# Dense head rows for the output projection and a second query block that ends in halves, in a fused pre-LN attention and gated feed-forward kernel

## The chip, the cores and the metric

The kernel runs on one NeuronCore of a Trainium2 chip, in one launch. The metric is the device time of that core in microseconds, as the median of several runs. The engines named below are TensorE (PE in the profile; its weight loads are PEld), VectorE (DVE), ScalarE (ACT), GpSimd (POOL) and SyncE (SP). SP issues nearly all DMAs of this kernel, one after the other, in the order in which the program was built.

## What is computed

One transformer block on x of 2048 rows and 640 columns (bf16), with 32 heads of 20 columns each, and a bilinear gated feed-forward layer of width 1728:

```python
def _A_ref(x, wqkv, wo):
    qkv = (x @ wqkv).reshape(B, S, 3, H, Dh).transpose(2, 0, 3, 1, 4)
    q, k, v = qkv[0], qkv[1], qkv[2]
    scores = jnp.einsum("bhqd,bhkd->bhqk", q, k) * (Dh ** -0.5)
    p = softmax(scores, axis=-1)
    o = jnp.einsum("bhqk,bhkd->bhqd", p, v)
    return o.transpose(0, 2, 1, 3).reshape(B, S, D) @ wo

def _B_ref(x, w_gate, w_up, w_down):
    return ((x @ w_gate) * (x @ w_up)) @ w_down

h  = x + _A_ref(layernorm(x), A_wqkv, A_wo)
h2 = h + _B_ref(layernorm(h), B_w_gate, B_w_up, B_w_down)
```

## The kernel before, in words

**Layout.** The heads are handled in eight groups of four (`NG = 8`, `HPG = 4`). Each head of 20 rows has a slot of 32 partitions, so a group fills the 128 partitions with 80 rows of use. The queries are cut into four blocks of 512 columns (`QB`), numbered 0 to 3.

**Attention.** A pass is one group against one query block or half of one. A list of passes, `segs`, is written out at the start: block 0 first (its first four groups in steps, while keys and values are still being made), then block 1 with all eight groups at 512 columns. Blocks 2 and 3 run their first two groups (`SPLIT_G = 2`) at 512 columns, and then the other six in two halves of 256: passes C and D for block 2, A and B for block 3. A half block's output can go on as soon as its own half is done.

The scores of a pass (keys on the partitions, queries on the columns) are cut into 683 tiles of 1536 columns in PSUM (`sc`, two buffers). For each tile, `emit_S` puts the score matmuls on TensorE and one exponential on ScalarE, into the SBUF tile `E`. Where `x_takes` says so, VectorE computes the exponential of the last 512 columns of a tile in four instructions (the tiles `xv`, `xt`, `xe`, called the x pieces here), and ScalarE's instruction is 1024 wide instead of 1536. In the last block `x_takes` asks `room()`: it adds up the TensorE work still to come by a table (`PE_NS`, `PART_NS`), compares it with the tiles that remain, and refuses a piece when less than `ROOM` is left over. `emit_AV` then multiplies `E` and `xe` with the values, into one PSUM tile `acc` per pass. The values carry a column of ones, so the sums of the exponentials come out as the 21st row of each slot.

**Normalising.** When a pass ends, VectorE copies `acc` to `asb`. `norm` sends the four rows of sums through DRAM (DMAs `sums`, `sums_all`), takes reciprocals four tiles later or more, sends these through DRAM again (`scr`, and four broadcasting DMAs `bc`), and seven tiles later VectorE multiplies (`times`) into `On[g]`, one tile for each group. The last groups of a half, named in `FAST`, do it on TensorE instead (`job_norm`).

**The rest of the block.** When all groups of a part (a block or half of one, list `due`) are normalised, `add_tail` queues three jobs: `job_out`, the output projection, which for each 128 rows and each half of the 640 columns (`out_mm`) sums over the eight group tiles, with `wo[g]` holding zeros between the slots; `job_glu`, the gate and up products over seven pairs of weight tiles (`glu_sum` at 512 columns, `glu_two` at 256); and `job_y`, the down projection and the store. A part of 512 columns loads each pair of weights once, a half block loads or holds them for its own 256 columns. `load_w` loads a pair while the one before is used, into two buffers. From the third block on, four of the seven pairs stay resident in the space of the old queries (`load_res`).

**Order.** The program is scheduled by the kernel itself while it is built: a loop over the tiles keeps estimates of each engine's time (`at`), and between score tiles `run_job` fills TensorE with chunks of the queued jobs as long as they fit before the next score tile is due. `later(n, fn)` does something n tiles later. `do(("spill", g), ...)` queues the copies of the queries to DRAM, which only a fallback at the end reads (`general`, entered when a check of the sums fails; it does not run on these inputs). When the tiles are done, `last_tail` finishes the last 256 rows on TensorE alone: `out_most` sums residual and groups 0 to 6, the last pass is normalised, `out_last` adds group 7, and then layer norm and feed-forward follow. The four halves of the down projection of the half block before (`held`) stand between them and hide the layer norm.

Of the kernel before, what the change touches and what calls it, by code (L numbers as in the profile page):

```python
# [29 lines left out]
NG = H // HPG  # L30
VS = DH + 1
# [11 lines left out]
SPLIT_G = 2  # L43
# [17 lines left out]
RES_STEPS = 3  # L61
WO_NS, SUMS_NS, ROOT_NS, ROWS_NS = 1500, 6000, 5000, 5000
# [6 lines left out]
PE_NS = {"out": 6000, "glu": 19500, "y": 3000}  # L69
PART_NS, TILE_NS, ROOM = 31500, 700, 5000  # L70
# [15 lines left out]
def kernel(  # L86
# [43 lines left out]
    wo = [const.tile([P, D], BF16, name=f"wo{g}") for g in range(NG)]  # L130
# [8 lines left out]
    On = [onp.tile([P, QB], BF16, name=f"on{g}") for g in range(NG)]  # L139
# [174 lines left out]
    def job_V(t, half):  # L314
        ps = bank()
        for c in range(KT):
# [12 lines left out]
            "C": (2, 0, HW), "D": (2, HW, HW), "A": (3, 0, HW), "B": (3, HW, HW)}  # L329
# [11 lines left out]
    TAILS = {0: [0], 1: [0], 2: [0, 2]}  # L341
    FAST = {("C", NG - 1), ("D", NG - 1), ("A", NG - 1), ("B", NG - 2)}
# [158 lines left out]
    def run_job(until):  # L501
# [9 lines left out]
        while cur["fresh"] or pe_free("F") + chunk() + SWITCH <= until:  # L511
            c = step()
            if c == FREE and cur["key"][0] not in ("spill", "load"):
                return run_job(until)
            if c in (None, NEXT, END, FREE):
                break
# [111 lines left out]

    def norm(s, asb):
# [11 lines left out]
        def back():  # L641
# [12 lines left out]
            def times(asb, bc, p, g, c0, w):  # L654
                nc.vector.tensor_tensor(On[g][:, c0:c0 + w], asb[:, 0:w], bc[:, 0:w], ALU.mult)
                done.add(("n", p, g))
# [32 lines left out]
    def job_norm(s, asb):  # L689
# [11 lines left out]
        nc.vector.tensor_tensor(On[g][:, c0:c0 + w], asb[:, 0:w], ps[:, 0:w], ALU.mult)  # L701
# [5 lines left out]
    def emit_AV(upto):  # L707
# [206 lines left out]
    def load_wo():  # L914
        for g in range(NG):
            nc.vector.memset(wo[g][:], 0.0)
            yield 230
            for j in range(HPG):
                h = HPG * g + j
                nc.sync.dma_start(wo[g][SLOT * j:SLOT * j + DH, :], A_wo[DH * h:DH * h + DH, :])  # L920
# [13 lines left out]
    def spill(g):  # L934
# [509 lines left out]
```

## Time and profile before

| What | Value |
|---|---|
| Median of 3 runs | 916.27 us (916.19 to 916.81) |
| The profiled execution | 916.05 us, span of its instructions 914.0 us |
| Granted TensorE clock, mean | 0.997 |
| Busy: PE, DVE, ACT, POOL | 817.5, 702.1, 866.2, 57.4 us |
| First and last exponential | from 15.6 to 869.9 us |
| DMA | 46.54 MB, mean 51 GB/s |

The span runs from the first to the last instruction; the time of a run has some 2 us more around it. Busy time of an engine counts its instructions and not its waits; a busy PE is not a PE at its peak. The chain that ended last is followed back from the last instruction, at each step to what released it. A line such as `L547 ACT ACTIVATE E<-sc` names the source line, the engine, the operation, and the tile written and read.

### The profile page before, as it was taken

How to read it: one execution, taken by the hardware profiler on the slowest of the kernel's cores; microseconds unless marked ns; L12 is line 12 of the kernel's file. 1: busy time of each engine (PE TensorE's matmuls, PEld its weight loads, DVE VectorE, ACT ScalarE, POOL GpSimd, SP SyncE). 2: the span in 40 equal slices, each digit the busy share in tenths (PEclk: the TensorE clock that was granted, in tenths of full speed). 3: DMA queues.
4: the chain of work that ended last, by engine and by line, in shares of the span. 5: the costliest groups of instructions: out<-in, count | busy, mean ns of one | idle time of the engine just before them, and what ended most of it. 6: DMA issues, size and time to landing. Idle time of an engine off the chain costs nothing.

```text
span 914.0 us, 20094 instructions
## 1 busy us (share of the span) xinstructions
PE 817.5 (89%) x8035; PEld 346.8 (38%) x8115; DVE 702.1 (77%) x1310; ACT 866.2 (95%) x719; POOL 57.4 (6%) x255
## 2 busy tenths in 40 slices
PE   8788999889989899899897888999998999998897
PEld 5233333222223222233232333434434445444575
DVE  8664349899999899899998999798998784542243
ACT  6999999999999999999999999999999999999931
POOL 4210000000001200000003000020001000010000
PEclk9999999999999999999999999999999999999999
DMA  6000011011025022212410022021411211201310
GB/s 195 17 14 1 1 27 27 14 24 37 4 61 149 13 71 72 64 49 90 160 28 14 20 70 68 19 54 49 117 51 42 73 28 51 57 15 50 80 44 18
DMA packets 74203, 46.54 MB, mean 51 GB/s; under 512 B 20380, under 2 KB 70440, under 8 KB 74104
## 3 DMA queue, kind: packets, MB, share of 16 engines
q1 hardware_dynamic: 74104, 45.20, 18.0%
q8 instruction: 65, 1.06, 0.5%
q14 instruction: 34, 0.28, 0.1%
HBM read 37.88 MB, written 7.30 MB: 49 GB/s over the span
## 4 chain that ended last, share of the span: by engine, by line
ACT 67%; issue 17%; PE 10%; DVE 4%; DMA 1%; POOL 1%; SPq 0%; ACTq 0%
ACT E L547 67%; PE sc L533 2%; PE f L1065 2%; PE f L1129 2%; PE acc L740 1%; DVE st L201 1%; PE mi L303 1%; PE mi L978 0%; PE f L1230 0%; PE mi L496 0%; DMA wu<-in_B_w_up_dram 0%; PE mi L317 0%; PE mi L1083 0%; DVE kT L310 0%; DVE vx L270 0%
## 5 line engine op out<-in xcount | busy, mean ns | idle before, releaser
L547 ACT ACTIVATE E<-sc 128x1536 bf16<-128x1536 f32 (+1 forms) x683 | 848.7, 1417 | 6.2 <-PE sc L533 5.9
L533 PE MATMUL sc<-qa,kT 32*128 32x512 bf16 (+1 forms) x1920 | 203.2, 340 | 28.6 <-ACT E L547 16.9
L533 PEld LDWEIGHTS <-kT 32*128 32x128 bf16 x2816 | 84.1, 91 | 244.6 <-issue 206.1
L740 PE MATMUL acc<-E,vx 128*32 128x256 bf16 (+1 forms) x2592 | 170.3, 326 | 1.7 <-DVE vx L270 1.2
L580 DVE TENSOR_SCALAR xv<-sc 128x512 f32<-128x512 f32 x167 | 115.0, 689 | 30.2 <-PE sc L533 26.5
L585 DVE SCALAR_TENSOR_TENSOR xe<-xt,xv 128x512 int16<-128x512 f32 x167 | 113.3, 682 | 1.0
L591 DVE SCALAR_TENSOR_TENSOR xt<-xt,xv 128x512 f32<-128x512 f32 x167 | 112.3, 681 | 0.5
L590 DVE SCALAR_TENSOR_TENSOR xt<-xv 128x512 f32<-128x512 uint16 x167 | 112.0, 683 | 0.3
L303 PE MATMUL mi<-lnT,wp 128*128 128x512 bf16 x279 | 83.3, 381 | 11.7 <-DVE qa L310 5.5
L740 PEld LDWEIGHTS <-vx 128*32 128x32 bf16 x2816 | 55.8, 95 | 66.4 <-issue 63.8
L533 PE MATMUL sc<-qb,kT 32*128 32x256 bf16 (+1 forms) x896 | 68.2, 288 | 8.1 <-ACT E L547 5.3
L1129 PE MATMUL mi<-wd,hh 128*128 128x320 bf16 x336 | 58.2, 301 | 1.6 <-DVE xr L1133 1.6
L740 PE MATMUL acc<-xe,vx 128*32 128x512 bf16 (+1 forms) x224 | 50.6, 332 | 0.0
L1129 PEld LDWEIGHTS <-hh 128*128 128x128 bf16 x448 | 38.7, 97 | 30.6 <-issue 18.7
L303 PEld LDWEIGHTS <-wp 128*128 128x128 bf16 x310 | 25.0, 97 | 55.9 <-issue 44.3
L310 DVE TENSOR_SCALAR kT<-mi,one_row 128x512 bf16<-128x512 f32 x30 | 22.5, 750 | 28.1 <-PE mi L303 24.7
L1065 PE MATMUL mi<-ln2T,wg 128*128 128x512 bf16 x128 | 38.0, 382 | 5.8 <-DVE u L270 5.2
L496 PE MATMUL mi<-kT,ident 128*128 128x512 bf16 x116 | 37.8, 386 | 5.5 <-DVE ln2T L270 1.0
L978 PE MATMUL mi<-wo,on 128*128 128x320 bf16 x224 | 40.5, 301 | 2.2 <-DVE xr L982 2.0
L1065 PE MATMUL mi<-ln2T,wu 128*128 128x512 bf16 x128 | 37.3, 382 | 4.3 <-DVE hh L1073 3.5
L1083 PE MATMUL mi<-ln2T,qa 128*128 128x256 bf16 x240 | 34.6, 274 | 4.1 <-DVE hh L1091 3.0
L207 POOL CAST mb<-mv 128x2 bf16<-128x2 f32 (+1 forms) x10 | 2.3, 231 | 528.6 <-DVE mv L202 410.9
(143 smaller groups left out, 645.0 us busy)
## 6 DMA issues: line engine op xcount, KB each, us to landing
wu<-in_B_w_up_dram SPq DMA_DIRECT2D x23, 320.0 KB
wg<-in_B_w_gate_dram SPq DMA_DIRECT2D x23, 320.0 KB
bc<-scr SPq DMA_DIRECT2D x80, 64.0 KB
qsp<-qa SPq DMA_DIRECT2D x8, 384.0 KB
xr<-in_A_x_dram SPq DMA_DIRECT2D x16, 160.0 KB
bc<-scr SPq DMA_DIRECT2D x76, 32.0 KB
out_dram<-xr SPq DMA_DIRECT2D x14, 160.0 KB
wd<-in_B_w_down_dram SPq DMA_DIRECT2D x13, 160.0 KB
```

The source lines that it names most:

```text
L303: nc.tensor.matmul(ps[:], lhsT=wslice(m, g, c), rhs=lnT[:, c, ch * QB:(ch + 1) * QB], start=(c == 0), stop=(c == KT - 1))
L496: nc.tensor.matmul(ps[:], lhsT=ident[:], rhs=kT[0][:, 0:BANK], start=True, stop=True)
L533: nc.tensor.matmul(sc[:, o:o + w], lhsT=kT[g][SLOT * j:SLOT * (j + 1), kt * P:(kt + 1) * P], rhs=q_of(g, b, c0, w)[SLOT * j:SLOT * (j + 1) ...
L547: exps = nc.scalar.activation(e[:, 0:n_act], sc[:, 0:n_act], ACT.Exp, bias=EXP_BIAS, scale=SM_SCALE)
L580: took = nc.vector.tensor_scalar(v[:], ps, X_SCALE, X_BASE, ALU.mult, ALU.max)
L585: nc.vector.scalar_tensor_tensor(e[:], t[:], X_R, v[:], ALU.mult, ALU.add)
L590: lambda: nc.vector.scalar_tensor_tensor(t[:], u, X_P, u, ALU.add, ALU.mult),
L591: lambda: nc.vector.scalar_tensor_tensor(t[:], t[:], X_Q, u, ALU.add, ALU.mult),
L740: nc.tensor.matmul(acc["t"][SLOT * j:SLOT * (j + 1), 0:w], lhsT=vx[kt][:, VS * h:VS * h + SLOT], rhs=e, start=(acc["n"][j] == 0), stop=(ac ...
L978: nc.tensor.matmul(ps[:, 0:HALF], lhsT=on[g][:, t * P:(t + 1) * P], rhs=wo[g][:, cs], start=(g == 0), stop=(g == NG - 1))
L1065: nc.tensor.matmul(ps[:, 0:n], lhsT=st["w", fp][k][:, c, f_cols(fp, f2)], rhs=st["ln2T"][:, c, c0:c0 + n], start=(c == 0), stop=(c == KT - 1))
L1129: nc.tensor.matmul(ps[:, 0:HALF], lhsT=st["hh"][f // 2][:, f % 2, t * P:(t + 1) * P], rhs=late["Wd"][f][:, cs], start=(f == 0), stop=(f == ...
```

## The change

It has two parts, and some constants that go with them.

**Dense rows.** The attention outputs of groups 0 to 6 (`OWN = 7`), 560 rows, are put one behind the other into five tiles of 128 rows (`NC = 5`) without the gaps of the slots. Group 7 keeps a slotted tile of its own (index 5), so the projection sums over six tiles instead of eight. VectorE multiplies a group below 7 into a staging tile `on` (two buffers), and SP moves each of its heads to the rows where they belong, in one DMA, or two where a head crosses from one tile to the next (`heads_of`). `times` marks such a group as done `ROWS_STEPS = 2` tiles later. `wo` is loaded in the same row order: five DMAs and four instead of 32, and two tiles zeroed instead of eight.

**Halves.** Block 1 runs its first four groups at 512 columns and then the other four in two halves (passes E and F), and its output, gate, up and down jobs come in two parts of 256 columns. Block 3 splits from its second group on instead of its third; block 2 stays as it was.

**Constants and order.** `room()` counts 4900 instead of 6000 for an output projection, and `ROOM` is 1000 instead of 5000. The spills of the queries come at fixed tiles (60 and four more for each group after block 0's part is queued) instead of in the queue of jobs. `asb` has three buffers instead of two. `rows_early`, the early load of the residual rows, waits for the second phase of memory to be open, and also covers the halves of block 1.

```diff
+OWN = NG - 1
+NC = -(-OWN * HPG * DH // P)
...
-SPLIT_G = 2
+SPLIT_G = {"1": 4, "2": 2, "3": 1}
...
+ROWS_STEPS, SPILL_AT = 2, 60
...
-PE_NS = {"out": 6000, "glu": 19500, "y": 3000}
-PART_NS, TILE_NS, ROOM = 31500, 700, 5000
+PE_NS = {"out": 4900, "glu": 19500, "y": 3000}
+PART_NS, TILE_NS, ROOM = 31500, 700, 1000
...
-    On = [onp.tile([P, QB], BF16, name=f"on{g}") for g in range(NG)]
+    On = [onp.tile([P, QB], BF16, name=f"on{c}") for c in range(NC + 1)]
...
+    nc.gpsimd.memset(On[NC - 1][:], 0.0)
...
+            "E": (1, 0, HW), "F": (1, HW, HW), "C": (2, 0, HW), "D": (2, HW, HW), "A": (3, 0, HW), "B": (3, HW, HW)}
...
-    segs += [("1", g, 0, NT, "only") for g in range(NG)]
-    for full, halves in ("2", "CD"), ("3", "AB"):
-        segs += [(full, g, 0, NT, "only") for g in range(SPLIT_G)]
-        segs += [(p, g, 0, NT, "only") for p in halves for g in range(SPLIT_G, NG)]
+    for full, halves in ("1", "EF"), ("2", "CD"), ("3", "AB"):
+        segs += [(full, g, 0, NT, "only") for g in range(SPLIT_G[full])]
+        segs += [(p, g, 0, NT, "only") for p in halves for g in range(SPLIT_G[full], NG)]
...
-    FAST = {("C", NG - 1), ("D", NG - 1), ("A", NG - 1), ("B", NG - 2)}
+    FAST = {("E", NG - 1), ("F", NG - 1), ("C", NG - 1), ("D", NG - 1), ("A", NG - 1), ("B", NG - 2)}
...
+    @contextmanager
+    def heads_of(g, c0, w):
+        if g == OWN:
+            yield On[NC][:, c0:c0 + w]
+            return
+        on = onp.tile([P, QB], BF16, name="on", tag="on", bufs=2)
+        yield on[:, 0:w]
+        for j in range(HPG):
+            a, end_ = DH * (HPG * g + j), DH * (HPG * g + j + 1)
+            while a < end_:
+                n = min(end_, (a // P + 1) * P) - a
+                r = SLOT * j + DH - (end_ - a)
+                nc.sync.dma_start(On[a // P][a % P:a % P + n, c0:c0 + w], on[r:r + n, 0:w])
+                a += n
...
             def times(asb, bc, p, g, c0, w):
-                nc.vector.tensor_tensor(On[g][:, c0:c0 + w], asb[:, 0:w], bc[:, 0:w], ALU.mult)
-                done.add(("n", p, g))
+                with heads_of(g, c0, w) as on:
+                    nc.vector.tensor_tensor(on, asb[:, 0:w], bc[:, 0:w], ALU.mult)
+                if g < OWN and now["i"] < n_tiles:
+                    later(ROWS_STEPS, lambda: done.add(("n", p, g)))
+                else:
+                    done.add(("n", p, g))
...
-                asb = parts[g] if kind == "copy" else nrm.tile([P, QB], F32, name="asb")
+                asb = parts[g] if kind == "copy" else nrm.tile([P, QB], F32, name="asb", bufs=3)
...
-            for g in range(NG):
-                nc.tensor.matmul(ps[:, 0:HALF], lhsT=on[g][:, t * P:(t + 1) * P], rhs=wo[g][:, cs],
-                                 start=(g == 0), stop=(g == NG - 1))
+            for c in range(NC + 1):
+                nc.tensor.matmul(ps[:, 0:HALF], lhsT=on[c][:, t * P:(t + 1) * P], rhs=wo[c][:, cs],
+                                 start=(c == 0), stop=(c == NC))
...
             for g in range(NG):
-                do(("spill", g), lambda g=g: spill(g))
+                later(SPILL_AT + 4 * g, lambda g=g: spill(g))
...
-            for g in range(NG - 1):
-                nc.tensor.matmul(ps[:, 0:HALF], lhsT=on[g][:, t * P:(t + 1) * P], rhs=wo[g][:, cs], start=False, stop=False)
+            for c in range(NC):
+                nc.tensor.matmul(ps[:, 0:HALF], lhsT=on[c][:, t * P:(t + 1) * P], rhs=wo[c][:, cs], start=False, stop=False)
...
-    due = [("0", range(NG), 0, [0, 1, 2, 3]), ("1", range(NG), 1, [0, 1, 2, 3]), ("C", range(SPLIT_G, NG), 2, [0, 1]),
-           ("D", range(SPLIT_G, NG), 2, [2, 3]), ("A", range(SPLIT_G, NG), 3, [0, 1])]
+    due = [("0", range(NG), 0, [0, 1, 2, 3]), ("E", range(SPLIT_G["1"], NG), 1, [0, 1]), ("F", range(SPLIT_G["1"], NG), 1, [2, 3]), ("C", range(SPLIT_G["2"], NG), 2, [0, 1]),
+           ("D", range(SPLIT_G["2"], NG), 2, [2, 3]), ("A", range(SPLIT_G["3"], NG), 3, [0, 1])]
```

More of the change, by code (lines that the diff above doesn't have):

```diff
@@ L2 @@
 from collections import deque
[L3 removed]
+from contextlib import ExitStack, contextmanager
 import concourse.bass as bass
@@ L129 @@
     huge = const.tile([P, 1], F32, name="huge")
-    wo = [const.tile([P, D], BF16, name=f"wo{g}") for g in range(NG)]
+    wo = [const.tile([P, D], BF16, name=f"wo{c}") for c in range(NC + 1)]
     N_SUMS = 16 * (NB * NG)
@@ L512, in run_job @@
             c = step()
-            if c == FREE and cur["key"][0] not in ("spill", "load"):
+            if c == FREE and cur["key"][0] != "load":
                 return run_job(until)
@@ L914, in load_wo @@
     def load_wo():
-        for g in range(NG):
[L916 to L920, printed above, removed]
+        for c in range(NC + 1):
+            rows = DH * HPG * OWN - c * P
+            if rows < P:
+                nc.vector.memset(wo[c][:], 0.0)
+                yield 330
+            if c < NC:
+                nc.sync.dma_start(wo[c][0:min(P, rows), :], A_wo[c * P:c * P + min(P, rows), :])
+            else:
+                for j in range(HPG):
+                    h = HPG * OWN + j
+                    nc.sync.dma_start(wo[c][SLOT * j:SLOT * j + DH, :], A_wo[DH * h:DH * h + DH, :])
             due = at["pe"] + WO_NS
@@ L1161, in rows_early @@
         key = b, ts[0]
-        if key in HELD_BY and key not in rows_in and all(("y",) + k in done for k in HELD_BY[key]):
+        if key in HELD_BY and key not in rows_in and ("open",) in done and all(("y",) + k in done for k in HELD_BY[key]):
             rows(b, ts)
```

33 lines of the change are left out of this document (18 added, 15 removed).

## The prediction

> **What bounds the kernel now.** I read the page first: busy shares, then the chain that ended last.
>
> ```profile
> span 914.0 us, 20094 instructions
> ...
> PE 817.5 (89%) x8035; PEld 346.8 (38%) x8115; DVE 702.1 (77%) x1310; ACT 866.2 (95%) x719; POOL 57.4 (6%) x255
> ...
> ACT 67%; issue 17%; PE 10%; DVE 4%; DMA 1%; POOL 1%; SPq 0%; ACTq 0%
> ```
>
> ScalarE is busy 95% of the span and carries 67% of the chain. The shares are an average, so the busy time by stretch comes next.
>
> ```profile
> core 0: us, PE busy (x) PEld busy (x) DVE busy (x) ACT busy (x) POOL busy (x), PEclk, DMA share, GB/s
> 200.00:250.00 50.00, 44.75 (x330) 13.39 (x335) 47.75 (x81) 50.00 (x43) 0.00 (x0) 1.00 0.12 27
> 500.00:510.00 10.00, 7.90 (x117) 3.11 (x117) 8.30 (x15) 9.51 (x9) 3.71 (x12) 0.83 0.09 25
> 550.00:600.00 50.00, 44.80 (x579) 19.34 (x584) 42.81 (x82) 50.00 (x42) 0.15 (x1) 1.00 0.17 44
> 650.00:700.00 50.00, 45.67 (x423) 20.08 (x423) 45.55 (x86) 50.00 (x42) 5.82 (x19) 1.00 0.33 85
> 750.00:800.00 50.00, 45.51 (x620) 25.24 (x615) 27.73 (x51) 49.16 (x39) 0.00 (x0) 1.00 0.19 50
> 800.00:850.00 50.00, 45.47 (x630) 24.61 (x635) 17.03 (x39) 50.00 (x38) 3.60 (x19) 1.00 0.12 30
> ```
>
> ACT is full in every stage, whether the passes are 512 columns wide (200 to 250) or 256 (550 to 600). So the length of the long middle is the ACT time of the exponentials plus the little that ACT waits:
>
> ```profile
> ACT E L547 <- PE sc L533: 5.9, 9, 1.1
> ```
>
> That is 5.9 us in nine waits. DVE takes a third of some exponential tiles away from ACT (the pieces x). In the last stage it is busy only 27.73 and 17.03 of 50 us: there the planner stops handing it pieces, because TensorE, at 45.5 of 50, would not finish the feed-forward work before the exponentials end. Freed TensorE time in the last block is worth something only through more such pieces. After the last exponential TensorE alone sets the end:
>
> ```profile
> 868.83 1.08 ACT E L547
> 869.91 0.04 issue
> 869.95 0.40 PE acc L740 x6
> ...
> 870.59 0.95 PE f L1230 x7
> ...
> 876.15 7.67 PE f L1129 x56
> ```
>
> **The change part by part.**
>
> *More pieces for DVE.* The order in which the built programs stand shows 683 exponential tiles in both, of which 168 are 1024 wide before and 179 after; the x pieces go from 167 to 178. By query block they go from 26, 55, 55, 31 to 27, 52, 55, 44. So 11 tiles more lose a third, 13 more of them in the last block, where DVE had room.
>
> ```profile
> L547 ACT ACTIVATE E<-sc 128x1536 bf16<-128x1536 f32 x515 | 717.2, 1520 | 5.7 <-PE sc L533 5.5
> L547 ACT ACTIVATE E<-sc 128x1024 bf16<-128x1024 f32 x168 | 178.2, 1100 | 0.5 <-PE sc L533 0.5
> ```
>
> 1520 - 1100 = 420 ns each, so 11 x 0.42 = **-4.6 us** on the path. Each piece costs DVE four instructions:
>
> ```profile
> L580 DVE TENSOR_SCALAR xv<-sc 128x512 f32<-128x512 f32 x167 | 115.0, 689 | 30.2 <-PE sc L533 26.5
> ```
>
> 13 x 4 x 0.69 = 36 us over the last 210 us or so. DVE had 22 and 33 us free in the two stretches above, so this is hidden; without that room the pieces would hold score banks and the gain would go.
>
> *Six products for eight in the output projection.* 28 halves in the middle and 4 at the end lose two matmuls each. One costs 0.95/7 = 0.136 us by the chain row of L1230. The 56 in the middle free 7.6 us of TensorE beside a full ACT: worth nothing themselves, they pay for the pieces. The 8 at the end lie on the path. The order also shows that 14 matmuls of the third down projection (L1129) leave the tail: 7 now stand before the last products with E, where TensorE waited for the last exponential
>
> ```profile
> 869.95 0.40 PE L740 MATMUL acc<-E,vx 128*32 128x256 bf16 x6 [0.52 <-ACT E L547]
> ```
>
> and 7 right behind them, still on the path. At 7.67/56 = 0.137 us each the tail loses 8 + 7 = 15 matmuls: **-2.0 us**. Bounds: the 7 moved ahead have only 0.52 us of wait to fill, so the rest may push the last products: -1.1 - 0.5 = -1.6 at the small end, -2.1 at the large one.
>
> *Halving.* Groups 4 to 7 of block 1 and group 1 of block 3 go through in halves. Scores and products with E of one tile, in 512 and in 256 columns:
>
> ```profile
> 424.65 0.39 PE L533 MATMUL sc<-qa,kT 32*128 32x512 bf16 x3
> ...
> 424.98 0.62 PE L740 MATMUL acc<-E,vx 128*32 128x512 bf16 x8
> ```
>
> ```profile
> 748.74 0.40 PE L533 MATMUL sc<-qb,kT 32*128 32x256 bf16 x6
> ...
> 761.26 0.62 PE L740 MATMUL acc<-E,vx 128*32 128x256 bf16 x16
> ```
>
> 0.39 against 0.40 and 0.62 against 0.62: over some 107 tiles 1 us of TensorE, beside ACT. Nothing.
>
> *Rows by DMA.* Each normalised group below 7 now goes to a staging tile, and four or five DMAs on SP put its heads into the dense rows: 193 issues. SP executes in order, and one place in this trace shows what a busy SP does:
>
> ```profile
> 752.18 0.32 SPq L649 DMA_DIRECT2D scr<-ri  x1
> ...
> 753.59 2.60 SPq L652 DMA_DIRECT2D bc<-scr  x4
> ...
> 756.23 0.42 SPq L1036 DMA_DIRECT2D wu<-in_B_w_up_dram  x1
> ...
> 759.21 0.50 SPq L636 DMA_DIRECT2D sums<-asb  x1
> 759.73 0.99 PEld L1083 LDWEIGHTS <-wu 128*128 128x128 bf16 x10 [1.31 <-DMA wu<-in_B_w_up_dram]
> 759.73 1.27 PE L1083 MATMUL mi<-ln2T,wu 128*128 128x256 bf16 x10 [1.03 <-DMA wu<-in_B_w_up_dram]
> 760.82 0.35 SPq L637 DMA_DIRECT2D sums_all<-sums  x1
> ...
> 761.44 1.45 ACT L547 ACTIVATE E<-sc 128x1536 bf16<-128x1536 f32 x1 [0.84 <-PE sc L533]
> 761.64 0.42 DVE L655 TENSOR_TENSOR on<-asb,bc 128x256 bf16<-128x256 f32 x1
> ```
>
> A weight load issued 4.05 us after the reciprocal's DMA landed late; TensorE stood 1.03 us and ACT lost 0.84 of it. Two new chances for the same:
>
> First, the output projection reads rows that may not be there. The loop counts a group as done ROWS_STEPS = 2 tiles after its multiply. A tile takes 50/42 = 1.19 us, so that is 2.4 us. What is needed: multiply 0.42, four issues ahead of the last, and 760.82 - 759.21 = 1.61 from the last issue to its landing. Issues cost 0.65 (2.60/4 above) or less:
>
> ```profile
> 429.42 1.71 SPq L652 DMA_DIRECT2D bc<-scr  x4
> ```
>
> 1.71/4 = 0.43. So 0.42 + 4 x 0.43 + 1.61 = 3.75 us, or 4.6 with the slow issue. Group 6 fills chunks 3 and 4, so three matmuls (0.4 us) run first: a wait of 3.75 - 2.4 - 0.4 = 0.95 to 1.8 us, of which ACT loses 0.2 less. By the build's order the gap between group 6's rows and the projection is the bare two tiles in two half blocks (block 2's second, block 3's first), three and four tiles in block 1's, ten or more elsewhere. Two full waits, and at three tiles 0 to 0.6: **+1.8 us**, between 0 (if DVE runs ahead of TensorE) and 3.8.
>
> [...]
>
> Second, block 1's two halves each load all their feed-forward weights, five pairs a half (block 2 holds four of seven resident), and use them about 4 to 7 tiles later instead of 9 to 12. The load above needed 759.73 - 756.23 = 3.5 us, or three tiles, so most are in time; I take one wait of 0.84 less a bit, **+0.5 us**, between 0 and 4 x 0.84 = 3.4, for those that stand right behind five row DMAs.
>
> *The rest costs nothing.* The zeroing on POOL stands before a wait that hides it:
>
> ```profile
> 3.75 0.30 POOL L190 MEMSET vx<- 128x12 bf16 x1
> 7.49 0.88 POOL L195 COPY wp<-E 128x640 bf16<-128x640 bf16 x1 [3.44 <-DMA E<-in_A_wqkv_dram]
> ```
>
> Fewer wo loads and memsets fall in a stretch where ACT is full (200 to 250), as do the q spills, moved ahead by some 40 tiles: only the fallback reads them, and SP then has 9 tiles between weight loads.
>
> **Sum.** -4.6 - 2.0 + 1.8 + 0.5 = -4.3 us. The profiled execution took 916.05 us (span 914.0 and 2.05 around it), 0.22 under the median 916.27 of the three runs, so 911.75 on its basis and 912.0 on the median's; I say **911.8 us**. The likeliest case's own range is 909.5 to 914.
>
> **Rivals.**
>
> *Clean.* DVE finishes its multiplies early, the rows are always there: 916.05 - 6.6 = 909.4 us. For it: DVE often stands idle in the last block. Against: the bare two tiles twice.
>
> *SP becomes the bound of the second block (slower).* Place: the halves of block 1, where ten pairs of weight loads, some 100 row and sum DMAs and the output stores queue in order. Every missed load costs 0.84 us of ACT as at 759.73, more if a store or a multiply ahead is late too. It decides from 6.6/0.84 = 8 such misses on; with all ten plus 3.8 us of row waits it is 916.05 - 6.6 + 8.4 + 3.8 = 921.7 us. Against: SP had room, and the one miss before stood behind a 2.60 us run of issues.
>
> *The pieces are not worth their ACT time.* The last block is then held by TensorE (45.5 of 50 us) and not by ACT: only the tail's 2.0 us remain, less 1.8 for rows: 915.9 us, no change. Against: ACT is at 50.00 there.
>
> *The array's clock falls more often.* Between 500 and 510 us the granted clock was 0.83 and ACT was busy 9.51 of 10: 0.49 us lost. The change takes away TensorE work (56 matmuls, and filler matmuls besides), so such dips could multiply; 13 of them would eat 6.4 us: about 916 us. The planner still places fillers, so I think this unlikely. [...]
>
> **How the numbers follow.** Forecast 0.55, clean 0.20, pieces worth nothing 0.08, SP as the bound 0.10 (a third of it still at no change, between 8 misses and fewer), clock 0.03, something else slower 0.04. A measurement here tells 0.2% (1.8 us) from no change: faster is below 914.4, slower above 918.1. Faster: 0.55 + 0.20 and a part of the SP case, 0.79; same: 0.12; slower: 0.09. Range 908.6 to 915.8: below, the clean case with the tail's and the pieces' own uncertainty; above, the forecast with its row waits at their upper end and three late loads (-6.6 + 3.8 + 3 x 0.84 = -0.3).
>
> **What would show it.** Right: 179 tiles of 1024 columns and ACT at 50 of 50 us with fewer us between the first and last exponential, by about 4.6 less new waits; the piece from the last exponential to the end shorter by 2.0; TensorE waits of about 1 us at the first output projection of block 2's second half and block 3's first, released by a DMA of the row tile. Wrong: ACT idle growing by over 4 us in total, PE waits for wu or wg in block 1's halves in more than two places, DVE waiting for DMAs of the staging tile, or a granted clock under 0.97 in more than one stretch of 50 us.

## The result, and the profile after

The changed kernel takes 923.78 us (median of 6 runs, 921.33 to 927.14) against 916.23 us (915.72 to 916.81) for the kernel before in the same comparison: a ratio of 1.0087 [1.0063, 1.0111]. It is 7.6 us slower, and 12 us above the forecast. The profiled execution took 922.27 us with a span of 920.0.

The page of the changed kernel, its busy shares and its chain, and the waits of ScalarE:

```profile
span 920.0 us, 21921 instructions
...
PE 816.3 (89%) x8743; PEld 366.3 (40%) x8810; DVE 728.0 (79%) x1367; ACT 864.2 (94%) x719; POOL 63.2 (7%) x256
...
ACT 47%; PE 23%; issue 13%; DVE 12%; DMA 2%; POOL 1%; SPq 1%; DVEq 0%; ACTq 0%
```

```profile
ACT E L550 <- PE sc L536: 11.2, 14, 1.8
...
ACT E L550 <- PE acc L763: 3.9, 7, 1.3
```

ScalarE is busy for 2.0 us less than before: the shorter tiles are there. But its share of the chain has dropped from 67% to 47%. It waits 11.2 us for scores where it waited 5.9, and there is a second row that the kernel before does not have: seven waits, 3.9 us, for products with E that still hold an E buffer. The same stretches as before (PE, PEld, DVE, ACT, POOL busy, granted clock):

```profile
core 0: us, PE busy (x) PEld busy (x) DVE busy (x) ACT busy (x) POOL busy (x), PEclk, DMA share, GB/s
200.00:250.00 50.00, 42.62 (x306) 12.76 (x308) 46.35 (x75) 47.84 (x41) 0.00 (x0) 0.98 0.10 29
550.00:600.00 50.00, 44.07 (x626) 23.89 (x626) 44.16 (x81) 49.23 (x42) 0.00 (x0) 1.00 0.39 98
750.00:800.00 50.00, 44.03 (x603) 22.40 (x605) 43.43 (x79) 48.28 (x40) 0.00 (x0) 1.00 0.16 42
800.00:850.00 50.00, 44.34 (x589) 21.29 (x594) 31.83 (x63) 47.63 (x38) 6.29 (x19) 0.97 0.13 31
```

ACT was at 50.00 in three of these four and now loses 0.8 to 2.4 us in each. VectorE has taken on its pieces in the last block (43.43 and 31.83 for 27.73 and 17.03). After the last exponential the chain reads:

```profile
876.45 1.08 ACT E L550
...
877.96 1.06 PE mi L1160 x7
...
879.16 0.68 PE f L1261 x5
...
883.81 5.77 PE f L1160 x42
```

Five products for seven in each half, 42 down matmuls for 56 with seven ahead of the projection. From the last exponential to the end of the span it is 42.5 us, 44.1 before.

The whole difference, between two profiled executions: the exponentials end at 877.5 us instead of 869.9, 7.6 later; the tail is 1.6 shorter; that is the 6.0 us of span. Eleven shorter tiles save 4.6 us of the first. ScalarE's idle time in front of exponentials, summed from the 61st tile on, rose from 1.7 to 11.5 us; 10.7 of these are waits of over 0.15 us, which the lines below show in brackets.

The rest, 2.4 us, lies in ScalarE's busy time, which fell by 2.0 us and not by 4.6. Without a gap, a whole exponential ends 1.34 us after the one before it in both kernels, and the two overlap by some 0.1 us. Behind a gap nothing overlaps, and it takes 1.45 us beside the gap. The changed kernel has 28 exponentials behind a gap where the kernel before has 8, so about 20 x 0.11 = 2.2 us. The exponentials themselves did not become slower.

**Where the 11.5 us lie.** The first wait of over 1 us:

```profile
243.71 0.69 DVE L674 TENSOR_TENSOR on<-asb,bc 128x512 bf16<-128x512 f32 x1
...
244.46 0.69 DVE L583 TENSOR_SCALAR xv<-sc 128x512 f32<-128x512 f32 x1
...
245.06 0.68 DVE L594 SCALAR_TENSOR_TENSOR xt<-xt,xv 128x512 f32<-128x512 f32 x1
...
245.71 0.69 DVE L775 COPY asb<-acc 128x512 f32<-128x512 f32 x1
246.46 0.61 PE L763 MATMUL acc<-E,vx 128*32 128x512 bf16 x8 [0.78 <-DVE asb L775]
246.93 4.17 ACT L550 ACTIVATE E<-sc 128x1536 bf16<-128x1536 f32 x3 [1.26 <-PE acc L763]
...
252.34 1.02 ACT L550 ACTIVATE E<-sc 128x1024 bf16<-128x1024 f32 x1 [1.24 <-PE sc L536]
```

A pass has ended, and its accumulator must be copied out before the next pass may use the bank. The copy stands in VectorE's order behind a normalising multiply and two steps of pieces. TensorE stands 0.78 us for it, and ScalarE, out of E buffers, 1.26. Seven waits for products with E at pass ends make the 3.9 us. At five of them (3.3 us) the products start within 0.1 us of the end of the copy, as here; at 613 and 814 us (0.6 us) the copy had ended 0.6 and 0.7 us before. The second wait of 1.24 comes 5 us later and has another cause, shown below. One of the two places where I had forecast a wait for rows:

```profile
794.45 0.41 DVE L674 TENSOR_TENSOR on<-asb,bc 128x256 bf16<-128x256 f32 x1
...
794.90 3.75 SPq L644 DMA_DIRECT2D on<-on  x5
...
799.93 0.43 PE L1009 MATMUL mi<-wo,on 128*128 128x320 bf16 x2 [1.12 <-DMA on<-on]
...
800.81 2.41 ACT L550 ACTIVATE E<-sc 128x1536 bf16<-128x1536 f32 x2 [1.78 <-PE sc L536]
...
803.72 1.02 ACT L550 ACTIVATE E<-sc 128x1024 bf16<-128x1024 f32 x1 [0.50 <-PE sc L536]
...
805.47 1.45 ACT L550 ACTIVATE E<-sc 128x1536 bf16<-128x1536 f32 x1 [0.72 <-PE sc L536]
```

Five issues take 3.75 us, 0.75 each. ScalarE loses 1.78 here and 1.21 at the other place (674 us, where TensorE waited 0.71 for the rows): 3.0. And again two more waits follow, 0.50 and 0.72. What they and the 1.24 have in common is the clock. Windows of 3.41 us before and after each fall of the granted clock, of the changed kernel:

```profile
245.07:248.48 3.41, 1.91 (x17) 1.00 0.07 18
248.48:251.89 3.41, 3.19 (x16) 0.50 0.06 11
...
661.50:664.91 3.41, 2.50 (x23) 1.00 0.05 9
664.91:671.74 6.83, 6.47 (x34) 0.50 0.60 165
798.03:801.44 3.41, 1.81 (x12) 1.00 0.04 8
801.44:804.85 3.41, 3.38 (x33) 0.50 0.03 5
```

(PE busy in us, its matmuls, granted clock, DMA.) TensorE was not idle ahead of these falls; it was busy 1.91, 2.50 and 1.81 of 3.41 us. One window at half clock follows, or two, in which the same work takes longer (the products of E over 512 columns take 619 ns on average from 248.48 to 251.89 us, 384 from 240 to 248.48) and the scores come late: 3.5 us of ScalarE behind the three. So 11.5 = 3.9 (pass ends) + 3.0 (rows) + 3.5 (behind clock falls) + 1.1 (small waits). This goes by the place of each wait; what a fall costs by itself is tested behind the third set.

The expectation of rows6, below, puts the middle fall down to the rows. But it came at 664.91 us, 9 us ahead of the row wait at 673.6. The window ahead of it holds two waits of TensorE, 0.46 us for VectorE (hh) and 0.70 us for ScalarE. That the change brought these is not shown.

### The profile page after: what moved, and what is told of

Its sections match the earlier page's. It is cut to its first block, busy times and chain, and to the rows that moved or that the text cites. A ratio compares the mean times of both kernels' runs of the same rounds, so it can differ in the third digit from the quotient of the medians.

```text
span 920.0 us, 21921 instructions
## 1 busy us (share of the span) xinstructions
PE 816.3 (89%) x8743; PEld 366.3 (40%) x8810; DVE 728.0 (79%) x1367; ACT 864.2 (94%) x719; POOL 63.2 (7%) x256
## 4 chain that ended last, share of the span: by engine, by line
ACT 47%; PE 23%; issue 13%; DVE 12%; DMA 2%; POOL 1%; SPq 1%; DVEq 0%; ACTq 0%
ACT E L550 47%; PE sc L536 6%; PE acc L763 4%; PE mi L1114 4%; PE mi L307 2%; PE f L1096 2%; PE f L1160 1%; DVE xt L593 1%; DVE xv L583 1%; PE mi L1009 1%; DVE xt L594 1%; DVE st L205 1%; PE mi L1160 1%; DVE u L1119 1%; DVE kT L314 1%
## 5 line engine op out<-in xcount | busy, mean ns | idle before, releaser
L550 ACT ACTIVATE E<-sc 128x1536 bf16<-128x1536 f32 (+1 forms) x683 | 846.6, 1399 | 16.0 <-PE sc L536 11.2
L536 PE MATMUL sc<-qa,kT 32*128 32x256 bf16 (+1 forms) x2176 | 204.0, 318 | 26.7 <-ACT E L550 16.6
L583 DVE TENSOR_SCALAR xv<-sc 128x512 f32<-128x512 f32 x178 | 122.7, 690 | 42.7 <-PE sc L536 40.7
L594 DVE SCALAR_TENSOR_TENSOR xt<-xt,xv 128x512 f32<-128x512 f32 x178 | 119.9, 682 | 0.5
L763 PEld LDWEIGHTS <-vx 128*32 128x32 bf16 x3136 | 66.4, 96 | 70.2 <-issue 67.5
L763 PE MATMUL acc<-xe,vx 128*32 128x256 bf16 (+1 forms) x283 | 55.5, 304 | 0.0
L1114 PE MATMUL mi<-ln2T,wg 128*128 128x256 bf16 x250 | 36.3, 274 | 6.7 <-DVE u L1119 6.2
L1114 PE MATMUL mi<-ln2T,wu 128*128 128x256 bf16 x250 | 36.5, 274 | 4.2 <-DVE hh L1122 3.6
L1009 PE MATMUL mi<-wo,on 128*128 128x320 bf16 x168 | 32.9, 305 | 6.2 <-DVE xr L1013 3.4
L1122 DVE TENSOR_TENSOR hh<-mi,u 128x512 bf16<-128x512 f32 x35 | 23.9, 684 | 15.5 <-PE mi L1114 15.2
L1119 DVE CAST u<-mi 128x512 bf16<-128x512 f32 x35 | 24.0, 687 | 12.0 <-PE mi L1114 12.0
```

The lines of the kernel that those rows point to most:

```text
L536: nc.tensor.matmul(sc[:, o:o + w], lhsT=kT[g][SLOT * j:SLOT * (j + 1), kt * P:(kt + 1) * P], rhs=q_of(g, b, c0, w)[SLOT * j:SLOT * (j + 1) ...
L550: exps = nc.scalar.activation(e[:, 0:n_act], sc[:, 0:n_act], ACT.Exp, bias=EXP_BIAS, scale=SM_SCALE)
L583: took = nc.vector.tensor_scalar(v[:], ps, X_SCALE, X_BASE, ALU.mult, ALU.max)
L594: lambda: nc.vector.scalar_tensor_tensor(t[:], t[:], X_Q, u, ALU.add, ALU.mult),
L763: nc.tensor.matmul(acc["t"][SLOT * j:SLOT * (j + 1), 0:w], lhsT=vx[kt][:, VS * h:VS * h + SLOT], rhs=e, start=(acc["n"][j] == 0), stop=(ac ...
L1009: nc.tensor.matmul(ps[:, 0:HALF], lhsT=on[c][:, t * P:(t + 1) * P], rhs=wo[c][:, cs], start=(c == 0), stop=(c == NC))
```

## The experiments

Idle is ScalarE's idle time in front of exponentials, as above; falls are stretches at clock 0.50 between 100 and 880 us of the profiled execution. Outside cold3 each lasts one window of 3.41 us or two; the seven of cold3 last 92 us together, 27 windows.

| run | median us | ratio to before [95%] | idle us | falls |
|---|---|---|---|---|
| before | 916.2 to 916.8 | 1 | 1.7 | 1 |
| changed | 923.78 | 1.0087 [1.0063, 1.0111] | 11.5 | 3 |
| rows6 | 926.36 | 1.0114 [1.0086, 1.0143] | 14.6 | 4 |
| dense | 921.68 | 1.0066 [1.0043, 1.0088] | 4.3 | 0 |
| cold3 | 929.37 | 1.0146 [1.0114, 1.0178] | 11.5 | 7 |
| warm2 | 936.71 | 1.0235 [1.0197, 1.0274] | 20.7 | 2 |
| pool | 925.63 | 1.0088 [1.0071, 1.0105] | 15.0 | 3 |
| copies | 916.86 | 1.0002 [0.9990, 1.0014] | 1.5 | 1 |
| broom | 915.78 | 0.9990 [0.9981, 1.0000] | 2.4 | 2 |
| late2 | 918.23 | 1.0014 [1.0004, 1.0024] | 4.8 | 2 |
| noends | 929.53 | 1.0163 [1.0118, 1.0209] | 17.0 | 3 |
| rows6pool | 918.20 | 1.0020 [1.0010, 1.0030] | 9.6 | 2 |
| consts | 920.41 | 1.0049 [1.0029, 1.0069] | 10.1 | 2 |
| late3 | 919.87 | 1.0036 [1.0019, 1.0053] | 5.5 | 1 |
| nudge | 916.48 | 1.0000 [0.9987, 1.0013] | 3.8 | 2 |
| nudge430 | 927.87 | 1.0119 [1.0098, 1.0141] | 11.1 | 2 |
| best1 | 921.85 | 1.0059 [1.0035, 1.0082] | 8.2 | 2 |
| dense6p | 926.25 | 1.0100 [1.0078, 1.0122] | 15.9 | 3 |
| nudge430s | 927.49 | 1.0123 [1.0104, 1.0143] | 8.7 | 2 |
| rows6sums | 934.30 | 1.0191 [1.0173, 1.0209] | 23.9 | 5 |

**First set: the two row waits, the halves, the clock.** rows6 is the changed kernel with `ROWS_STEPS` 6 for 2.

> The changed kernel with ROWS_STEPS 6 instead of 2: a group counts as done six tiles after its multiply, so that its rows have landed before the output projection reads them; 177 pieces instead of 178. Row theory (the two TensorE waits on row DMAs, 0.71 and 1.12 us, start the loss at 660 to 675 and at 800 us): no wait on the row tile left, those two stretches of halved clock gone, ACT idle between exponentials down from 11.5 by about 5 us, time about 918.5 us. Clock theory without rows (low TensorE load anywhere lets the granted clock fall to 0.50 for 3.4 us, and the rows are only one cause): the waits go, but about as many stretches at half clock stay at other places, time 921 to 924 us. Planner theory (estimates of VectorE are short, ACT waits at pass ends): nothing changes but the two waits, 921 us.

No wait for rows is left, and the kernel is no faster. Its profile has TensorE waiting for late weight loads in their place:

```profile
PE mi L1114 <- DMA wu<-in_B_w_up_dram: 5.6, 4, 2.5
```

The longest of the four, 2.5 us at 486 us, is found in rows6pool below as well, where SyncE issues no row; the other three (0.8, 0.5 and 1.8 us) are not.

dense has the dense rows without the halves of block 1 and of group 1 of block 3; it keeps the change's constants.

```diff
-SPLIT_G = {"1": 4, "2": 2, "3": 1}
+SPLIT_G = {"2": 2, "3": 2}
...
+    segs += [("1", g, 0, NT, "only") for g in range(NG)]
```

> Dense rows alone: block 1 whole and block 3 split from its third group as before, everything else as in the changed kernel; 171 pieces. Row theory: block 2's and 3's half parts still start two tiles after the last rows, so the waits stay and the time lies near 921 us. If the halves are what costs: 913 us or less (4 pieces more than before, -1.7 us, and the shorter tail, -1.6 us). Clock theory: more stretches at half clock than before's single one, since the projection gives TensorE less to do; 2 or 3, and 917 to 922 us.

Half of its idle, 2.2 us, are the same two pass ends at 220 and 247 us. In its profiled execution no clock fall follows them. That execution took 919.75 us at a mean clock of 0.997; others of the same kernel took 925.2 and 924.28 at 0.992. The difference between 0.997 and 0.992 is 918 x 0.005 / 0.5 = 9 us at half clock, and it goes with about 5 us of time.

cold3 is the kernel before without its filler matmuls (in two places, `ident` against `kT[0]`, results that nobody reads); warm2 is the changed kernel with each of them issued twice.

> The kernel before, without its filler matmuls (the ones on the identity in front of score tiles and between jobs); all else stands in the same order, outputs are the same. Clock theory: the granted clock falls to 0.50 in stretches of 3.4 us several more times, each with 0.5 to 3 us of ACT idle around it; 5 to 10 stretches, time 920 to 940 us. If a fall of the clock is cheap by itself (0.49 us as the one in the profile of before) and the waits around it are what counts: 5 to 10 stretches but under 921 us. If fillers matter for nothing: 916 us.

> The changed kernel with each filler matmul issued twice, in the same order and without being counted in the kernel's own estimates; 0.2 us more of TensorE at each of 29 and 0.4 at each of 50 places. Clock theory: fewer stretches at half clock (0 to 2 instead of 3), spread of the runs under 3 us, time 917 to 921 us. Row theory: the waits at the two projections stay and so do the two stretches behind them, 920 to 924 us. Planner theory: fillers only take time from a TensorE that is already late, 924 us or more.

Without fillers the clock falls seven times and 13 us are lost: the fillers of the kernel before do work. But 11.5 us of idle over 27 windows are only about 0.4 us a window, an estimate that takes all of the idle for the clock's; in the changed kernel it is 3.5 us over four. A window at half clock has no fixed price. Twice as many still leave two falls and add 9 us of idle: in the middle TensorE has no time to give.

**Second set: SyncE's load, the pieces.** pool issues the row DMAs from GpSimd (`nc.gpsimd.dma_start`). copies adds to the kernel before five DMAs of 20 rows behind each normalising multiply, to a scratch in DRAM.

> Changed kernel, its 193 row DMAs issued by GpSimd instead of SyncE; the planned order of tiles and pieces is the same. Theory A (the changed kernel loses its time through short TensorE waits of several kinds, each of which may bring a stretch of granted clock 0.50 that costs ScalarE 2 to 3 us): the rows are as late as before at the projections, the waits for the copy of the accumulator at pass ends stay, so 921 to 926 us, with 2 to 4 stretches at 0.50 before the last exponential. Theory B (SyncE's 0.75 us for each of 193 issues is what hurts, about 145 us of its queue): the loads and the sums come in time, ScalarE's waits fall from 11.5 us to under 6, and the time to 916 to 918 us.

> Kernel before, plus five DMAs of 20 rows on SyncE behind each normalising multiply, out to a DRAM scratch that nobody reads: the issue load of the dense rows without anyone waiting for them; planned order as before, 167 pieces. Theory A: SyncE has room, so at most one or two late weight loads, 916 to 918 us, unless one of them brings a stretch of clock 0.50 (2 to 3 us more). Theory B: weight loads and sums come late behind the issues as in the changed kernel, 919 us or more.

copies costs nothing, but it does not carry the whole load. One of its DMAs, from SBUF to DRAM, holds SyncE for 0.33 us (median of 195; 66 us together), a row DMA of the changed kernel, from SBUF to SBUF, for 0.71 us (median of 193; 138 us together). So half of the load does no harm in the order of before; the whole of it was not tried there. In pool GpSimd began its issues 3.2 us after the multiply had ended, and the projection waited longer than in the changed kernel:

```profile
673.20 0.42 DVE L674 TENSOR_TENSOR on<-asb,bc 128x256 bf16<-128x256 f32 x1
...
676.85 2.54 POOL L644 DMA_DIRECT2D on<-on  x5 [11.62 <-DVE xe L588]
679.05 0.42 PE L1009 MATMUL mi<-wo,on 128*128 128x320 bf16 x1 [1.75 <-DMA on<-on]
```

The page names a piece step (xe) that ended at 676.6 as the releaser; why GpSimd waited for that one was not tried. From 600 to 700 us its row DMAs landed a median of 1.8 us after their issue (1.9 over all 193):

```profile
on<-on POOLq DMA_DIRECT2D x17, 10.0 KB, 1.8
```

broom is the kernel before with `ROOM` 1000 for 5000. late2 has dense rows in block 3 only: five loads put the dense weight over the slotted one once block 2's projection has read it, and `ROOM` is 1000.

```diff
+        if b < LAST_B or g == OWN:
+            yield On[g][:, c0:c0 + w]
+            return
...
+    def dense_wo():
+        for c in range(NC):
+            n = min(P, DH * HPG * OWN - c * P)
+            nc.sync.dma_start(wo[c][0:n, :], A_wo[c * P:c * P + n, :])
```

> Kernel before with ROOM 1000 for 5000 and nothing else: 173 pieces instead of 167, all six new ones in the last block. If a piece is worth its 0.42 us of ScalarE there (the term of the prediction): 916.3 - 2.5 = 913.8 us. Theory C (the extra pieces crowd VectorE, so that copies and score banks come late, and the pieces give back what they gain): 916 us or more, with new ScalarE waits of 2.5 us or more in the last block.

> Kernel before through blocks 0 to 2; only block 3 has dense rows (five chunks of the dense weight are loaded over the slotted ones when block 2's projection has read them; 65 row DMAs, counted as done 6 tiles after the multiply) and ROOM 1000 with out at 4900: 173 pieces, planned order unchanged up to tile 568 of 683. Theory A: nothing disturbs the first 570 tiles; six pieces save 2.5 us, and eight matmuls less behind the last exponential 1.1 us: 912.7 us, range 911 to 915. Theory C: the pieces give their gain back and only the tail's 1.1 us stay: 915.2 us or more. If any dense row at all is harmful (Theory B): 917 us or more.

Six pieces that should be worth 2.5 us brought 0.9 [0.0, 1.7]. late2 missed its forecast by 5.5 us. The multiply of group 6 waited 3.36 us for its one staging tile, and a reciprocal waited 2.49 us for the sums.

**Third set: repair.** noends forbids the two pieces that stand two tiles before the last tile of the passes whose copies come at 220 and 247 us (`i not in (147, 168)` in `x_takes`). rows6pool joins rows6 and pool. consts is the changed kernel with `ROOM` 5000 and `out` 6000. late3 gives late2 two staging tiles of 256 columns.

> Changed kernel with two pieces forbidden: tiles 147 and 168, each the last but one of its pass (176 pieces instead of 178, about 0.84 us more for ScalarE). Theory A (a piece in the last tile but one of a pass lets VectorE's copy of the accumulator come late, and the stall that follows may bring a stretch of clock 0.50): ScalarE's waits of 0.90 us at 220 and 1.26 us at 247 and the stretch at 248 with its 1.24 us vanish, 3.4 us, so 923.8 - 3.4 + 0.8 = 921.2 us, range 919 to 924. Rival D (the waits come from whatever the planner puts there, and move on): new waits of the same size within some ten tiles, 923.8 to 926 us.

> Changed kernel with ROWS_STEPS 6 for 2 and the row DMAs issued by GpSimd: no projection waits for rows, and SyncE's queue is as free as before the change. Theory A, item by item: the row waits (3.0 us of ScalarE at 674 and 801) and the stretches of clock 0.50 around them (2.2 us) go, and the late weight loads of the run with six steps (5.6 us of TensorE) do not come: 918 to 921 us. Rival D (an order this tight finds another stall for each that is taken away): 923 to 927 us, with as much idle time of ScalarE as the changed kernel's 11.5 us.

> Changed kernel with the old constants of the last block (ROOM 5000, out at 6000): 174 pieces instead of 178, the planned order differs in the last block alone. If a piece is worth 0.42 us: 923.8 + 1.7 = 925.5 us. Theory C (the added pieces crowd VectorE and give their gain back): 921 to 923.8 us, with less idle time of ScalarE after 760 us than the changed kernel's 4 us.

> As the run with dense rows in block 3 alone, but with two staging tiles of 256 columns for one of 512 (groups 0 and 1 are multiplied in two halves): the multiply that waited 3.36 us for the staging tile does not wait. Theory A: its 0.80 us of ScalarE at 868 and with it the lengthened end go, about 918.2 - 1.5 = 916.7 us, and no faster than the kernel before with ROOM 1000 (915.8 us) by more than the tail's 1.1 us. Rival: the staging tile was not it, 918 us again.

noends did what it should at its place: no wait at 220 or 247, no fall at 248. And it was 5.7 us slower, with falls at 310, 368 and 809 that the changed kernel does not have. It is not the changed kernel with two waits less: the planner answered with 42 tiles changed between whole and shortened. rows6pool has the same planned order as rows6 and differs only in the queue; 8.2 us apart, the largest gain of all. consts removes four pieces and is 3.4 us faster, though the intervals overlap a little; in its profile the last exponential ends where it did (877.9 us) and the part behind it is shorter, 40.1 us for 42.5. In these two executions the four pieces bought nothing. late3 lost the wait for the staging tile and found a reciprocal that stood 2.96 us for the sums, with a fall of the clock behind it.

**One stall, with and without a fall.** Six of the runs have the same tiles up to the wait of 1.26 us shown above (247 us in the changed kernel), and the same wait, to 0.01 us. The windows of the clock, laid out from each run's own falls, cut this stall differently:

| run | TensorE busy in the two windows around the stall, of 3.41 us | next window | ScalarE's wait three tiles on, us |
|---|---|---|---|
| changed | 2.90, 1.91 | half clock | 1.24 |
| rows6 | 2.89, 1.92 | half clock | 1.21 |
| pool | 2.89, 1.91 | half clock | 1.13 |
| rows6pool | 2.89, 1.92 | half clock | 1.23 |
| consts | 2.56, 2.78 | full clock | none |
| best1 | 2.42, 2.40 | full clock | none |

consts has the tiles of the changed kernel up to the 602nd. (dense and warm2 have the wait as well, and none three tiles on; dense has no fall to lay the windows from, warm2 has more filler matmuls in them.) So at this place the fall is what costs the second 1.2 us, and where the window lies, not the stall, decides whether it comes. Part of what one profiled execution shows of a repair is therefore luck.

**Fourth set: is it the change, or any new order?** nudge and nudge430 are the kernel before, where the planner is told that zeroing a tile of wo costs 330 or 430 ns.

```diff
-            yield 230
+            yield 330
```

> Kernel before, where the planner is told that zeroing a tile of the output weights costs VectorE 330 ns instead of 230 (the changed kernel's figure). No instruction is added or removed but for one piece (168 instead of 167); 143 tiles change between whole and shortened. Rival D (an order that has not been tried and chosen finds new TensorE stalls, and clock stretches at 0.50 behind them): 919 to 925 us, ScalarE idle 4 to 12 us against 1.7. Theory A (the loss belongs to the change's own operations): 916.4 - 0.4 = 916.0 us, range 915.5 to 917.5.

> As nudge with 430 ns: 165 pieces, 150 tiles changed. Theory A: 916.4 + 0.8 = 917.2 us. Rival D: 919 to 926 us, and not the same as nudge.

> Changed kernel with ROWS_STEPS 6, the row DMAs issued by GpSimd, and the old constants of the last block: 174 pieces. If the two cures add: 918.2 - 3.4 = 914.8 us, which would beat the kernel before (916.4). If they do not add, because the constants' gain was that of another order: 917 to 919 us.

> Dense rows alone (block 1 whole, block 3 in halves from its third group, old constants) with ROWS_STEPS 6 and the row DMAs issued by GpSimd: 174 pieces. If the halves cost something of their own, this is 1 to 3 us below best1: 913 to 915 us. If they cost nothing, the same as best1 within 1 us.

(dense6p has dense's constants, the change's own, and not the old ones that its expectation names; it differs from best1 in those too.) nudge is level with before. nudge430 is 11.6 us slower with no operation added and two pieces less, more than the whole change lost. The cures do not add: best1 is 3.7 us above rows6pool. Where nudge430 loses most:

```profile
267.42 9.29 SPq L956 DMA_DIRECT2D wd<-in_B_w_down_dram  x14
276.82 0.51 SPq L636 DMA_DIRECT2D sums<-asb  x1
279.57 0.33 SPq L637 DMA_DIRECT2D sums_all<-sums  x1
...
281.18 0.25 DVE L647 RECIPROCAL ri<-sums_all 128x16 f32<-128x16 f32 x1 [5.00 <-DMA sums_all<-sums]
...
283.62 1.23 PE L978 MATMUL mi<-wo,on 128*128 128x320 bf16 x4 [4.59 <-DVE xr L982]
...
285.50 1.45 ACT L547 ACTIVATE E<-sc 128x1536 bf16<-128x1536 f32 x1 [5.19 <-PE sc L533]
```

The same stretch of the kernel before:

```profile
266.81 0.50 SPq L636 DMA_DIRECT2D sums<-asb  x1
268.50 0.34 SPq L637 DMA_DIRECT2D sums_all<-sums  x1
...
273.35 9.22 SPq L956 DMA_DIRECT2D wd<-in_B_w_down_dram  x14
```

There the sums leave ahead of the 14 loads, and their second half 1.7 us later. In nudge430 the loads come first; the sums queue behind all of them, VectorE starts nothing else while it stands 5.00 us at the reciprocal, and a projection result (xr), for which TensorE waits 4.59 us, comes only behind it. The last two runs took the two DMAs of the sums off SyncE:

```diff
-        nc.sync.dma_start(sums[:], asb[DH:P:SLOT, 0:w])
-        nc.sync.dma_start(r16, sums[:].rearrange("j (c f) -> (j c) f", f=n))
+        nc.gpsimd.dma_start(sums[:], asb[DH:P:SLOT, 0:w])
+        nc.gpsimd.dma_start(r16, sums[:].rearrange("j (c f) -> (j c) f", f=n))
```

> As nudge430, with the two DMAs of the sums' round trip issued by GpSimd instead of SyncE; the planned order is the same. Theory E (SyncE executes in order, and what the planner's order puts behind a run of loads comes late; VectorE and TensorE wait, and the clock falls behind them): the reciprocal at 281 no longer waits 5.0 us, ScalarE's 5.2 us and most of the 4 us around the two stretches of clock 0.50 go, so 927.9 - 8 = 920 us, range 917 to 923. Rival D (the order itself is bad, whichever wait shows first): 924 us or more.

> Changed kernel with ROWS_STEPS 6, and the row DMAs and the two DMAs of the sums' round trip issued by GpSimd; order as in the run with six steps. Theory E: the weight load at 484 us is no longer queued behind the round trip, the 2.5 us wait of TensorE and 1.9 us of ScalarE there vanish, 918.2 - 1.9 = 916.3 us, range 914 to 918; that would be level with the kernel before. Rival D: another wait in its place, 918 us or more.

Neither helped. In nudge430s the sums were issued at 269.92, at once, and still landed late:

```profile
266.97 8.33 SPq L956 DMA_DIRECT2D wd<-in_B_w_down_dram  x14
269.92 0.58 POOL L636 DMA_DIRECT2D sums<-asb  x1 [4.42 <-DVE asb L752]
275.18 0.57 POOL L637 DMA_DIRECT2D sums_all<-sums  x1 [4.68 <-DMA sums<-asb]
279.65 0.25 DVE L647 RECIPROCAL ri<-sums_all 128x16 f32<-128x16 f32 x1 [3.93 <-DMA sums_all<-sums]
```

```profile
268.00:272.00 4.00, 2.91 (x25) 0.99 (x25) 3.68 (x7) 4.00 (x5) 0.58 (x1) 1.00 1.06 286
272.00:276.00 4.00, 4.00 (x37) 1.27 (x34) 3.14 (x6) 4.00 (x5) 0.57 (x1) 1.00 1.08 364
```

The DMA engines were full (shares 1.06 and 1.08, 286 and 364 GB/s), and 8 KB needed 5.0 us for what takes 1.7 in the kernel before. So at this place it is the transfers that are crowded: issuing the sums from GpSimd did not help. In rows6sums the sums waited on GpSimd, and the reciprocals waited for them six times, 10.2 us in all.

## Why the prediction was wrong

*Pieces, -4.6.* The count (179 tiles of 1024 columns) and 420 ns each were right. That they stay gained was wrong: broom kept 0.9 [0.0, 1.7] of 2.5 us, and consts was no slower without four of them.

*Tail, -2.0.* Right, at the small end of its bounds: 1.6.

*Halves, 0.* Not told apart: the changed kernel is 2.1 us above dense with overlapping intervals, and best1, with halves, 4.4 us below dense6p, which has other constants too. The 7.6 us of TensorE that the projection was to free are there (40.5 us of products before, 32.9 after), but TensorE's whole busy time fell by 1.2 us only: other work of the changed kernel took the rest. How much of that is the halves' was not separated.

*Rows, +1.8 (0 to 3.8).* Both places and the mechanism were right, the size was not. An issue takes 0.75 us where I took 0.43 to 0.65, from DMAs of another kind (bc). With 0.75 the formula would have given 0.42 + 4 x 0.75 + 1.61 - 2.4 - 0.4 = 2.2 us at each place; TensorE waited 0.71 and 1.12. That these come to 1.8, the very term, is luck. ScalarE lost 3.0 us, more than TensorE waited, where I had it lose less. The term stops there: what the same stall does to the clock was not in it.

*Weights, +0.5.* No wait of this kind came in the changed kernel while the weights of block 1's halves were used. TensorE waits 0.5 us for wu once, at 657 us, and ScalarE loses nothing by it (busy 4.50 of 4.50 us from 657.0 to 661.5). In rows6 TensorE waited 5.6 us.

*The rest, nothing.* Wrong by 3.9 us: the waits at pass ends. The prediction looks for VectorE's added work in the last block alone, hidden by its free time there, and does not ask anywhere what stands in VectorE's order behind a multiply and the pieces.

*The clock, a rival at 0.03 and 0.49 us a fall.* I took the price from the one fall before, and expected falls from less TensorE work. At 248 and 801 us they come right behind short stalls of TensorE, 0.78 us for the copy and 1.12 for the rows, and the three falls cost 3.5 us beside the stalls. The sign I named for it was met: the clock is 0.93 from 650 to 700 us, and from 800 to 850 it is 0.966 (3.41 of 50 us at half), which the profile prints as 0.97.

*The step that failed* is the sum's allowance for new waits of ScalarE: 2.3 us, from rows and weights. The two profiled executions differ by 9.8 us of waits, and by 2.4 us more for exponentials that a gap keeps from overlapping. What was put at nothing is the waits at pass ends (3.9), the clock behind the stalls (3.5) and the lost overlap (2.4); the rows were 1.2 us too small. Less the 1.7 us of waits that the kernel before has, with the small waits (1.1), the shorter gain at the tail (0.4) and no wait for weights (-0.5), this is 10.3 of the 10.5 us by which the profiled execution missed the forecast's -4.3.

Beneath these lies the assumption of the sum itself: that each edit could be priced against the order of before, with the rest held. The planner gives a new order (tiles change between whole and shortened from the 148th on), and nudge430 shows that a new order alone can cost 11.6 us, nudge that it can cost nothing. SP as the bound, with its 921.7 us, came closest in time, but not for its reason: in the changed kernel TensorE waits for weights once, for 0.5 us. The load is not cleared by that. Taking the rows off SyncE gained 8.2 us in one order (rows6 against rows6pool) and nothing in another (the changed kernel against pool), and copies carries only half of it.

What stays open: how much of the 7.6 us belongs to the operations and how much to the order. The repairs did not add, and in two of them (consts and best1) the clock's windows lay elsewhere against the same stall, so no split can be read from them. Why the planner's new order has the copies and rows where it has them was not taken apart. No run beat the kernel before by more than the measurement tells (broom, 0.9990).

## What to carry to other kernels

Where a planner places everything, price a change by the order it produces and not by its own instructions: list, for the new order, what stands behind each DMA round trip (5.00 us of VectorE at the reciprocal of nudge430) and each copy (1.26 us of ScalarE at 247 us of the changed kernel). A perturbation that changes little but the order (nudge430) tells how large the lottery is, and belongs at the start of such a study. In the changed kernel, with TensorE 89% busy, the stall at 247 us cost ScalarE 1.26 us and, behind the clock's fall, 1.24 more: ask of a stall whether it pulls a clock window under.

## What the hardware showed

*The clock's falls, as these traces have them.* In the changed kernel the first fall lasts 3.41 us (clock 0.50 from 248.48 to 251.89), and the falls begin whole numbers of such windows apart: 664.91 - 248.48 is 122 and 801.44 - 664.91 is 40 times 3.413 us. Laying that grid over the 19 profiled executions of the table that have a fall, between 100 and 865 us at full clock: of 43 windows in which TensorE was busy up to 60% (rounded to whole per cent), 39 were followed by one at half clock; of 61 between 60 and 72%, 5; of 4095 above, 3 (some matmul records may be missing). In the kernel before and the changed one alone these are 3 of 3, 0 of 6 and 1 of 432. By that, at TensorE's 89% about (0.89 - 0.60) x 3.41 = 1 us of stall within one window would be enough, an estimate. Where the grid lies differs from run to run, so the same stall is doubled in one run and not in the next, as the table behind the third set shows: 1.24 us follow the 1.26 in the changed kernel, none in best1. The runs of one kernel spread with the clock, too, though only one of each was profiled: the changed kernel took 921.33 us at a mean clock of 0.995 and 927.14 at 0.990.

*Small DMAs.* A row DMA of the changed kernel (some 20 rows, from SBUF to SBUF) held SyncE for 0.71 us (median of 193), one of 20 rows from SBUF to DRAM in copies for 0.33 us (median of 195). In nudge430s an 8 KB transfer took 5.0 us, three times the 1.7 us of the kernel before, while weight loads filled the DMA engines (shares 1.06 and 1.08).
